# Lightning attention and a low-rank mixer on one core: the attention steps regrouped by TensorE tile shape

## The chip, the cores and the metric

The kernel runs on one core of one Trainium2 chip. The metric is the device time of one execution in microseconds (us). Of the kernel before there are three runs, 670.92, 672.37 and 673.74 us, so the median is 672.37 us.

## The reference

Two blocks follow each other. The first is causal linear attention with a decay per head, on q, k, v of 4 batches, 8 heads, 768 tokens and 64 columns. The reference does it by blocks of 64 tokens; in short:

```python
for each block of tokens:
    intra = ((q k^T) * Dmask) v            # Dmask = lam^(i-j) for i >= j, else 0
    inter = (q * lam^(pos+1)) kv_state
    out   = intra + inter
    kv_state = lam^block * kv_state + (k * lam^(block-1-pos))^T v
```

The heads' columns are put side by side, which gives x of 4 x 768 tokens x 512 columns. The second block mixes tokens through a product of rank 32 and then has a layer over the columns:

```python
h   = x^T @ U @ V                          # over the 768 tokens, rank 32
u   = x + h^T
out = u + max(u @ w_ch1, 0) @ w_ch2        # 512 -> 2048 -> 512
```

Everything is float32 in and out.

## The kernel before

Attention takes 128 tokens of one batch a step, all eight heads at once: 24 steps s, six to a batch (NT = 6, c = s % NT is the step's place in its batch). In a step the heads lie in pairs (HP = 4 pairs a, x = 0 or 1 within the pair), and `half` is the upper or lower 64 partitions. Its parts are:

- `prep(s)`: TensorE transposes q and k (L355, into pq and pk), four 128x128 transposes each, and ScalarE copies the results to qt and kt (L358). Step 0 does it in two parts.
- `scale(s)`: GpSimd makes qs = qt times powers of the decay (L383), and ks, the scaled keys of the next step (L372).
- `scores(s)`: products of kt and qt into the two banks pss (L400); for s over 6 on tiles of 64x64, before that of 64x128.
- `masked(s)`: VectorE multiplies pss by the decay mask, one instruction for each x, into sm (L409).
- `inter(s)`: qs times the state kv into the two banks px, on 64x64 tiles (L441); not in a batch's first step.
- `intra(s)`: sm times v, added into the same px, on 128x64 tiles (L453); ScalarE then copies px to xs[s], the step's 128x512 piece of x (L459).
- `state(s)`: ks times v into the bank pkv (L418); VectorE adds the faded old state to give kv[s + 1] (L424, L426). `fade` is the fading, four ScalarE instructions (L392). A batch's last step has no state.

Behind the attention, by seven steps, runs the mixer's first part on finished batches. `low(b)` forms U^T x of a whole batch in pp (L470). `low_rows(b)` and the three pieces that `next_of_low(b)` runs one by one split its rows into a high and a low part and spread them over four groups of 32 partitions of p_hl (L490, L496, L501, L505). `mix(s)` multiplies by V and VectorE adds the sum onto xs[s], which makes it u (L515, L518). `turn(s)` transposes u (L532), stores u to DRAM on the SP queue (L535), and VectorE splits the transposed u in two parts (ut L537, u_hl L548); `turned` is the rest of that split, on ScalarE (L551) and GpSimd (L552).

Beside this, `aside(s)` runs single pieces of the preparation of weights (U, V and the first column blocks of w_ch1): VectorE instructions (L149 to L224, L615 to L626), with ScalarE ones that are held back in a list and issued at `late` (L167, L168, L212).

The order of all instructions in this stage is written out by hand, in the list `pieces` (L562 to L584); each engine takes its own in that order. For the steady step it gives TensorE: transposes of q and k of s + 1, mix, intra(s), state(s), scores(s + 1), inter(s + 1), transposes of u. PSUM has eight banks: pss and px two each, and one each with the tags pq, pk, pu and pt. Loads of q, k and v are issued on the SP queue where a buffer is freed (q and v have three, k four).

After the last attention step come the first product (`hidden`, L733 and L743), into which the last batch's turns and mixes are put at written slots (the list `rest`, L788), and the second product (`product`, L866 to L870). Both use fp32r matmuls of 128x128 by 512 columns.

## Time and profile before

| what | value |
|---|---|
| median of three runs | 672.37 us |
| profiled execution | 671.76 us, span 669.9 us, TensorE clock 1.00 |
| start of the first product (L733) | 119.06 us |
| 0 to 119.06 us, busy | TensorE 116.84, VectorE 96.76, ScalarE 76.63, GpSimd 70.58 us; DMA share 0.86 |
| 119.06 to 144 us, busy | TensorE 24.94, VectorE 21.44, ScalarE 13.63 us |
| 144 us to the end, busy | TensorE 522.13 of 525.90, VectorE 379.29 us |

A matmul's record contains its way through the array, so that records of a stream overlap; what one costs in a stream is the time from one start to the next. The chain of work that ended last gives such times for a run of instructions: a line has its start, the time it held the chain, the engine, the tile written, the line of the code and the number of records. The page and the list of groups give per group the number of records, busy time and mean duration, and behind the bar the engine's idle time just ahead of them. In the order of time a line shows start, length from first start to last end, engine, line and operation, and the tiles.

### The profile page before, as it was taken

How to read it: one execution, taken by the hardware profiler on the slowest of the kernel's cores; microseconds unless marked ns; L12 is line 12 of the kernel's file. 1: busy time of each engine (PE TensorE's matmuls, PEld its weight loads, DVE VectorE, ACT ScalarE, POOL GpSimd, SP SyncE). 2: the span in 40 equal slices, each digit the busy share in tenths (PEclk: the TensorE clock that was granted, in tenths of full speed). 3: DMA queues.
4: the chain of work that ended last, by engine and by line, in shares of the span. 5: the costliest groups of instructions: out<-in, count | busy, mean ns of one | idle time of the engine just before them, and what ended most of it. 6: DMA issues, size and time to landing. Idle time of an engine off the chain costs nothing.

```text
span 669.9 us, 13328 instructions
## 1 busy us (share of the span) xinstructions
PE 663.9 (99%) x5204; PEld 544.5 (81%) x5204; DVE 497.5 (74%) x873; ACT 277.5 (41%) x517; POOL 112.1 (17%) x92
## 2 busy tenths in 40 slices
PE   9999999999999999999999999999999999999997
PEld 8898989788888888888888888888888888888886
DVE  4689989877999777777797265787586775865864
ACT  4675866454655444444454122232322322322320
POOL 4455767240000000000000000030030300300300
PEclk9999999999999999999999999999999999999999
DMA  8999894354776655555577989854363353543421
GB/s 188 219 234 248 212 246 141 102 196 153 262 251 233 215 202 202 201 202 204 204 282 273 326 308 392 282 184 136 95 220 95 118 196 95 160 155 94 163 90 63
DMA packets 131776, 131.29 MB, mean 196 GB/s; under 512 B 81346, under 2 KB 89794, under 8 KB 131714
## 3 DMA queue, kind: packets, MB, share of 16 engines
q1 hardware_dynamic: 130512, 130.05, 61.1%
q8 instruction: 41, 0.67, 0.4%
q10 hardware_dynamic: 1202, 0.39, 0.2%
q14 instruction: 21, 0.17, 0.1%
HBM read 80.09 MB, written 50.33 MB: 195 GB/s over the span
## 4 chain that ended last, share of the span: by engine, by line
PE 97%; DVE 1%; DMA 1%; ACT 0%; issue 0%; DVEq 0%; ACTq 0%
PE pz L733 27%; PE pz L868 13%; PE pz L866 13%; PE pd L743 13%; PE pd L870 13%; PE px L453 4%; PE pss L400 3%; PE put L532 2%; PE pq L355 2%; PE pkv L418 1%; PE pk L355 1%; PE px L441 1%; DMA qraw<-in_q_dram 1%; PE pp L470 1%; PE pu L515 1%; PE idle L343 0%
## 5 line engine op out<-in xcount | busy, mean ns | idle before, releaser
L733 PE MATMUL pz<-u_hl,w 128*128 128x512 f32 x768 | 190.5, 397 | 0.0
L733 PEld LDWEIGHTS pz<-u_hl,w 128*128 128x128 f32 x768 | 144.0, 188 | 35.4 <-issue 0.4
L868 PE MATMUL pz<-w_hl,m 128*128 128x512 f32 x384 | 151.1, 396 | 0.0
L866 PE MATMUL pz<-w_hl,m 128*128 128x512 f32 x384 | 150.9, 396 | 0.0
L870 PE MATMUL pd<-w_d,m 128*128 128x512 f32 x384 | 149.5, 396 | 0.0
L849 ACT ACTIVATE m<-mt 128x512 fp32r<-128x512 f32 x96 | 60.5, 632 | 196.4 <-PE pd L870 140.9
L850 DVE SCALAR_TENSOR_TENSOR m<-rm,m 128x512 fp32r<-128x512 f32 x96 | 71.4, 746 | 53.8 <-ACT m L849 53.5
L895 POOL TENSOR_TENSOR o<-o,u 128x512 f32<-128x512 f32 x20 | 29.9, 1527 | 447.4 <-DVE o L891 447.4
L748 DVE SCALAR_TENSOR_TENSOR r<-pd,r 128x512 f32<-128x512 f32 x96 | 61.8, 686 | 53.6 <-ACT r L739 43.5
L743 PE MATMUL pd<-u_d,w 128*128 128x512 f32 x384 | 98.6, 397 | 0.0
L739 ACT ACTIVATE r<-pz 128x512 f32<-128x512 f32 x96 | 52.2, 596 | 93.2 <-PE pz L733 92.5
L868 PEld LDWEIGHTS pz<-w_hl,m 128*128 128x128 f32 x384 | 72.3, 188 | 17.7
L870 PEld LDWEIGHTS pd<-w_d,m 128*128 128x128 f32 x384 | 72.3, 188 | 17.6
L866 PEld LDWEIGHTS pz<-w_hl,m 128*128 128x128 f32 x384 | 72.3, 188 | 17.6
L743 PEld LDWEIGHTS pd<-u_d,w 128*128 128x128 f32 x384 | 72.1, 188 | 17.3
L851 DVE SCALAR_TENSOR_TENSOR m<-m 128x512 fp32r<-128x512 f32 x96 | 69.1, 721 | 0.9
L848 DVE TENSOR_SCALAR mt<-rm 128x512 uint32<-128x512 uint32 x96 | 46.1, 481 | 26.4 <-DMA rm<-r_d 26.1
L409 DVE TENSOR_TENSOR sm<-pss,mask 128x512 f32<-128x512 f32 x48 | 30.9, 685 | 7.3 <-PE pss L400 7.1
L212 ACT CAST w<-wt 128x512 fp32r<-128x512 f32 x32 | 19.9, 620 | 30.6 <-DVE wt L209 23.4
L383 POOL TENSOR_TENSOR qs<-qt,powq 128x512 f32<-128x512 f32 x20 | 25.9, 1297 | 20.3 <-ACT qt L358 19.8
L453 PEld LDWEIGHTS px<-vraw,sm 128*64 128x64 f32 x768 | 24.6, 137 | 5.5 <-issue 2.3
L453 PE MATMUL px<-vraw,sm 128*64 128x64 f32 x768 | 28.1, 225 | 0.1
(88 smaller groups left out, 682.1 us busy)
## 6 DMA issues: line engine op xcount, KB each, us to landing
r_d<-r SPq DMA_DIRECT2D x96, 256.0 KB, 2.4
rm<-r_d SPq DMA_DIRECT2D x96, 256.0 KB, 2.7
words<-in_moe_w_ch_dram SPq DMA_DIRECT2D x30, 512.0 KB, 4.5
w_d<-w SPq DMA_DIRECT2D x16, 768.0 KB, 3.3
w_hl<-w_d SPq DMA_DIRECT2D x16, 512.0 KB, 6.3
vraw<-in_v_dram SPq DMA_DIRECT2D x24, 256.0 KB, 5.0
u_d<-x_nat SPq DMA_DIRECT2D x24, 256.0 KB, 3.7
u<-u_d SPq DMA_DIRECT2D x24, 256.0 KB, 4.0
```

What stands on the lines that cost most here:

```text
L453: nc.tensor.matmul(out=px[half[t], x, a, :], lhsT=sm[:, x, a, half[t]], rhs=vr[:, 2 * a + x, :], start=(first and a == 0), stop=(a == HP - 1),
L733: nc.tensor.matmul(out=acc[g][0], lhsT=w[:, n, ct, :], rhs=uhl[g][:, n, ct, :], start=(ct == 0 and n == 0), stop=(ct == CT - 1 and n == 1),)
L739: nc.scalar.mul(rs[g], acc[g][0], 4096.0 + 1.0)
L743: nc.tensor.matmul(out=acc[g][1], lhsT=w[:, 2, ct, :], rhs=ud[g][:, ct, :], start=(ct == 0), stop=(ct == CT - 1),)
L748: nc.vector.scalar_tensor_tensor(rs[g], acc[g][1], 4096.0, rs[g], ALU.mult, ALU.add)
L848: nc.vector.tensor_scalar(t.bitcast(U32), r.bitcast(U32), HI, None, ALU.bitwise_and)
L849: nc.scalar.activation(out=m[:, 0], in_=t, func=AF.Relu)
L850: nc.vector.scalar_tensor_tensor(m[:, 1], r, 0.0, hi, ALU.max, ALU.subtract)
L851: nc.vector.scalar_tensor_tensor(m[:, 2], hi, E, low, ALU.mult, ALU.subtract)
L866: nc.tensor.matmul(out=pz, lhsT=m[:, 0, cols], rhs=hl[:, 0], start=first, stop=False)
L868: nc.tensor.matmul(out=pz, lhsT=m[:, 1, cols], rhs=hl[:, 1], start=False, stop=end)
L870: nc.tensor.matmul(out=pd, lhsT=m[:, 2, cols], rhs=dd, start=first, stop=end)
```

## The change

What it does, part by part:

- Transposes of q, k and (in the attention stage) u are done by halves of the tokens: each takes 64 partitions to 128, on a 64x128 tile, with the two halves written to two different banks. There are sixteen for q and k and eight for u in place of eight and four. q and k share the two banks `pqk`.
- `scores` uses 64x128 tiles in all steps.
- `mix` is four matmuls of 64 rows and 256 columns. p_hl holds the rows of the first 256 columns in its upper half and those of the others in its lower half, and the columns of p_hl hold the high and the low part. The sum is added onto xs by `mixed`, apart from the matmuls.
- `turn` and `mix` share two banks `pm`: the left half holds the transposes, the right half the sums. `turn` is one step later than before and works on the piece mixed a step earlier. Its two VectorE instructions are issued by `split`, and `store` is the DMA of u.
- `intra` comes first on px and is ordered by x; `inter(s)` follows `state(s)` in the same step, adds onto intra's sums and ends with the copy to xs.
- `state` writes to the first of the banks `pqk`.
- `low(b)` runs at the end of the batch's last step, in the banks px, and (but for the last batch) is followed by four ScalarE copies of its rows; `low_rows` works on 32x512 and the lows on 32x256 pieces.
- The mix of the batch's last piece before the first product (piece 17) moves from the first product into the last attention step. The turn of piece 16 moves from slot 4 to slot 7 of the first product.

The core of the diff:

```diff
-    def turn_half(s, a0, name):
-
-        ts, tag = (qts, ("pq", "pt")) if name == "q" else (kts, ("pk", "pu"))
+    def turn_parts(s, a0):
+
+        n = HP // parts(s)
         if a0 == 0:
-            ts[s] = att.tile([P, HP, P], FP32, tag=name + "t", bufs=2, name=name + "t")
-        n = HP // parts(s)
-        pt = one_bank([P, n, P], "p" + name, tag[a0 > 0])
-        for a in range(a0, a0 + n):
-            nc.tensor.transpose(
-                out=pt[:, a - a0, :], in_=raw[s, name][:, 2 * a : 2 * a + 2, :], identity=ident
-            )
-        nc.scalar.copy(ts[s][:, a0 : a0 + n, :], pt)
+            for ts, name in ((qts, "qt"), (kts, "kt")):
+                ts[s] = att.tile([P, HP, P], FP32, tag=name, bufs=2, name=name)
+        pt = two_banks("pqk", "px" if a0 else "pqk")[:, :, 0 : 2 * n * D]
+        pt = pt.rearrange("p t (n a i) -> p t n a i", n=2, a=n)
+        for i, name in enumerate("qk"):
+            for a in range(n):
+                for t in range(2):
+                    nc.tensor.transpose(
+                        out=pt[:, t, i, a, :],
+                        in_=raw[s, name][half[t], 2 * (a0 + a) : 2 * (a0 + a) + 2, :],
+                        identity=ident[half[t], half[t]],
+                    )
+        for i, ts in enumerate((qts, kts)):
+            nc.scalar.copy(
+                ts[s][:, a0 : a0 + n, :].rearrange("p a (t i) -> p t a i", t=2), pt[:, :, i]
+            )

     def prep(s):
         for a0 in range(0, HP, HP // parts(s)):
-            for name in "qk":
-                turn_half(s, a0, name)
+            turn_parts(s, a0)
...
-                for rows in half if s > NT else [slice(0, P)]:
-                    nc.tensor.matmul(
-                        out=pss[rows, x, a, :], lhsT=kt[half[x], a, rows],
-                        rhs=qt[half[x], a, :], start=True, stop=True,
-                    )
+                nc.tensor.matmul(
+                    out=pss[:, x, a, :], lhsT=kt[half[x], a, :], rhs=qt[half[x], a, :],
+                    start=True, stop=True,
...
-            pkv = one_bank([P, HP, D], "pkv", "pk")
+            pkv = two_banks("pkv", "pqk")[:, 0, 0 : HP * D].rearrange("p (a e) -> p a e", a=HP)
...
-    def inter(s):
+    def intra(s):

         st[s]["px"] = both = two_banks("px", "px")
         px = both[:, :, 0 : HP * D].rearrange("p x (a e) -> p x a e", a=HP)
-        if s % NT == 0:
-            return
-
-        for a in range(HP):
+        sm, vr, alone = st[s]["sm"], raw[s, "v"], s % NT == 0
+        for x in range(2):
+            for a in range(HP):
+                for t in range(2):
+                    nc.tensor.matmul(
+                        out=px[half[t], x, a, :], lhsT=sm[:, x, a, half[t]],
+                        rhs=vr[:, 2 * a + x, :], start=(a == 0), stop=(alone and a == HP - 1),
+                    )
+
+    def inter(s):
+
+        px = st[s]["px"][:, :, 0 : HP * D].rearrange("p x (a e) -> p x a e", a=HP)
+        for a in range(HP if s % NT else 0):
             for x in range(2):
                 for t in range(2):
                     nc.tensor.matmul(
                         out=px[half[t], x, a, :], lhsT=st[s]["qs"][half[x], a, half[t]],
-                        rhs=kv[s][half[x], a, :], start=(a == 0), stop=False,
-                    )
-
-    def intra(s):
-        first = s % NT == 0
-        sm, vr, px = st[s]["sm"], raw[s, "v"], st[s]["px"]
-        px = px[:, :, 0 : HP * D].rearrange("p x (a e) -> p x a e", a=HP)
-        for a in range(HP):
-            for x in range(2):
-                for t in range(2):
-                    nc.tensor.matmul(
-                        out=px[half[t], x, a, :], lhsT=sm[:, x, a, half[t]],
-                        rhs=vr[:, 2 * a + x, :], start=(first and a == 0), stop=(a == HP - 1),
+                        rhs=kv[s][half[x], a, :], start=False, stop=(a == HP - 1),
                     )
         pool, tag = (att, "x10") if s % 10 == 5 else (x_pool, "x")
         xs[s] = pool.tile([P, C], FP32, tag=tag, name="x_nat")
         nc.scalar.copy(xs[s].rearrange("p (a x e) -> p x a e", a=HP, x=2), px)
-
+        del st[s]
...
-        tag = "pq" if b else "pu"
-        pp = one_bank([P, P], "pp", tag) if b < B - 1 else bank([P, P], "pp", "b2")
+        pp = two_banks("pp", "px")[:, 0, 0:P] if b < B - 1 else bank([P, P], "pp", "b2")
         for c in range(NT):
             for g in range(G):
                 nc.tensor.matmul(
@@ -472,53 +473,100 @@
                     rhs=xs[b * NT + c][:, g * P : (g + 1) * P],
                     start=(c == 0), stop=(c == NT - 1),
                 )
-        pps[b] = pp
+        if b == B - 1:
+            pps[b] = pp
+            return
+        pps[b] = rows_f = tmp("p_f")[0:R]
+        for g in range(G):
+            nc.scalar.copy(rows_f[:, g * P : (g + 1) * P], pp[g * R : (g + 1) * R])
...
+        rows_f = pp
+        nc.vector.tensor_scalar(t.bitcast(U32), rows_f.bitcast(U32), HI, None, ALU.bitwise_and)
+        wide = [slice(x * 2 * P, (x + 1) * 2 * P) for x in range(2)]
+
+        def place(g, low):
+            return p_hl[g * R : (g + 1) * R, wide[low]]
+
+        def spread():
+            for g in range(G):
+                nc.scalar.copy(place(g, 0), t[:, wide[g // 2]])

         def low_part():
-            for rows, cols in own:
+            for x in range(2):
                 nc.vector.tensor_tensor(
-                    out=l[:, cols], in0=pp[rows], in1=t[:, cols], op=ALU.subtract
+                    out=place(2 * x, 1), in0=rows_f[:, wide[x]], in1=t[:, wide[x]],
+                    op=ALU.subtract,
                 )

-        def spread():
-            nc.scalar.copy(h, t)
-            nc.scalar.copy(h2, t)
-
         def spread_low():
-            nc.scalar.copy(l2, l.bitcast(FP32))
+            for x in range(2):
+                nc.scalar.copy(place(2 * x + 1, 1), place(2 * x, 1).bitcast(FP32))

         pps[b] = [spread, low_part, spread_low]

...
+    def both_halves(s):
+        if s not in pms:
+            pms[s] = two_banks("pm", "pqk" if s == NS - NT - 1 else "pm")
+        return pms[s]
+
     def mix(s):
         b, c = divmod(s, NT)
-        pu = one_bank([P, C], "pu", "pu") if s < NS - NT - 1 else bank([P, C], "pu", "b2")
-        nc.tensor.matmul(
-            out=pu, lhsT=v_hl[:, c * P : (c + 1) * P], rhs=p_hl, start=True, stop=True
-        )
+        weights = v_hl[:, c * P : (c + 1) * P]
+        if b < B - 1:
+            pm = both_halves(s)[:, :, 2 * P :]
+            for low in range(2):
+                for x in range(2):
+                    nc.tensor.matmul(
+                        out=pm[:, x], lhsT=weights[half[x]],
+                        rhs=p_hl[half[x], low * 2 * P : (low + 1) * 2 * P],
+                        start=(low == 0), stop=(low == 1),
+                    )
+            return
+        pu = bank([P, C], "pu", "b2")
+        nc.tensor.matmul(out=pu, lhsT=weights, rhs=p_hl, start=True, stop=True)
         nc.vector.tensor_tensor(out=xs[s], in0=pu, in1=xs[s], op=ALU.add)
+
+    def mixed(s):
+        pm, x = pms.pop(s)[:, :, 2 * P :], xs[s].rearrange("p (x e) -> p x e", x=2)
+        nc.vector.tensor_tensor(out=x, in0=pm, in1=x, op=ALU.add)

+    def store(s):
+        nc.sync.dma_start(out=u_d[s], in_=xs[s])

...
-        nc.vector.tensor_tensor(out=low, in0=pt, in1=t, op=ALU.subtract)
+        pt = both_halves(s + 1)[:, :, 0 : 2 * P].rearrange("p t (c i) -> p t c i", i=D)
+        for ct in range(CT):
+            for n in range(2):
+                nc.tensor.transpose(
+                    out=pt[:, n, ct, :], in_=xs[s][half[n], ct * P : (ct + 1) * P],
+                    identity=ident[half[n], half[n]],
+                )
+        del xs[s]
...
+        t = tmp("ut").rearrange("p (c n) -> p c n", n=P)
+        split_t = parts_of(t.bitcast(U32))
         turned[s] = rest

-
-
-
-
-    pieces = [("prep", 0), ("scale", 0), ("scores", 0), ("inter", 0), ("masked", 0)]
+        def split():
+            nc.vector.tensor_scalar(split_t, pt.bitcast(U32), HI, None, ALU.bitwise_and)
+            nc.vector.tensor_tensor(
+                out=parts_of(low), in0=pt, in1=parts_of(t), op=ALU.subtract
+            )
+
+        splits[s] = split
+
+    splits = {}
+
+    pieces = [("prep", 0), ("scale", 0), ("scores", 0), ("masked", 0)]
     for s in range(NS):
         b, c = divmod(s, NT)
         done = s - NT - 1
         more = s + 1 < NS
-        step = [("prep", s + 1), ("scale", s + 1)] * more + [("fade", s)] * (c == 1)
+        turns = done > 0 and (done - 1) // TG < FG
+        mixes = 0 <= done < NS - NT - 1
+        step = [("prep", s + 1), ("scale", s + 1)] * more
+        step += [("turn", done - 1)] * turns + [("mix", done)] * mixes
+        step += [("mix", done + 1)] * (not more)
+        step += [("next_of_low", b - 1)] * (c == 0 and b > 0)
+        step += [("fade", s)] * (c == 1)
         step += [("late", s - 1)] * (s in (NT, 3 * NT - 1))
-        step += [("mix", done)] * (0 <= done < NS - NT - 1)
-        step += [("low", b - 1)] * (c == 0 and b > 0)
-        step += [("low_rows", b - 1)] * (c == 0 and b > 0)
-        step += [("intra", s)]
+        step += [("split", done - 1)] * turns + [("next_of_low", b - 1)] * (c == 0 and b > 0)
+        step += [("mixed", done)] * mixes + [("mixed", done + 1)] * (not more)
         step += [("next_of_low", b - 1)] * (c == 0 and b > 0)
-        step += [("late", s)] * (s < NT - 1 or s == NT) + [("state", s)]
-        step += [("next_of_low", b - 1)] * (c == 0 and b > 0)
+        step += [("intra", s), ("state", s), ("inter", s)]
+        step += [("late", s)] * (s < NT - 1 or s == NT)
         step += [("turned", done - 1)] * (done > 0) + [("late", s)] * (done >= 0)
-        step += [("next_of_low", b - 1)] * (c == 0 and b > 0)
         step += [("scores", s + 1)] * more
+        step += [("low", b)] * (more and c == NT - 1)
         step += [("aside", s)] * (s >= 2 * NT)
-        step += [("inter", s + 1), ("masked", s + 1)] * more
+        step += [("masked", s + 1)] * more
+        step += [("low_rows", b)] * (more and c == NT - 1)
         step += [("fade", s + 1)] * (more and c > 0)
         step += [("aside", s)] * (s < 2 * NT)
-        step += [("turn", done)] * (done >= 0 and done // TG < FG)
+        step += [("store", done)] * (done >= 0 and done // TG < FG)
         pieces += step
...
+    pl = two_banks("pl", "pss")[:, 0, 0:H]
     keep_busy(2)
-    pl = one_bank([P, H], "pl", "pt")
...
-        (0, 4, "turn", c0 - 2), (0, 6, "mix", c0 - 1), (0, 9, "low", b), (0, 14, "low_rows", b),
+        (0, 7, "turn", c0 - 2), (0, 9, "low", b), (0, 14, "low_rows", b),
```

For the last batch, `low_rows`, `mix` and `turn` keep their old form inside the first product.

## The prediction

> **What bounds the kernel now.** I read the page first, for which engine fills the span:
>
> ```profile
> span 669.9 us, 13328 instructions
> PE 663.9 (99%) x5204; PEld 544.5 (81%) x5204; DVE 497.5 (74%) x873; ACT 277.5 (41%) x517; POOL 112.1 (17%) x92
> ```
>
> TensorE carries 97% of the chain that ended last. By the chain, the first product (L733) starts at 119.06 us; only what lies before it, and one mix just after, is touched. From 144 us on TensorE has no gap and runs the same matmuls in both kernels. So the next view is the chain, one attention step at a time:
>
> ```profile
> 78.16 0.59 PE put L532 x4
> 78.75 0.44 PE pq L355 x4
> 79.18 0.44 PE pk L355 x4
> 79.62 0.23 PE pu L515
> 79.85 1.08 PE px L453 x32
> 80.93 0.47 PE pkv L418 x16
> 81.40 1.19 PE pss L400 x32
> 82.59 0.51 PE px L441 x31
> ```
>
> A step is TensorE end to end; the neighbouring one (73.42 to 78.16) has 1.03 and 0.46 in the last two rows and makes 4.74 us. Like work costs 0.59 when it follows another tile shape (put) and 0.44 when it doesn't: a change of shape is 0.15 us, and the step has three (into put, px L453, pss).
>
> Next the groups by shape, for the durations of one:
>
> ```profile
> L355 PE MATMUL pq<-ident,qraw 128*128 128x128 f32 x96 | 15.5, 284 | 0.3 <-DMA qraw<-in_q_dram 0.2
> L400 PE MATMUL pss<-qt,kt 64*128 64x128 f32 x112 | 8.9, 305 | 0.0
> L400 PEld LDWEIGHTS pss<-qt,kt 64*128 64x128 f32 x112 | 7.6, 207 | 0.7 <-ACT kt L358 0.3
> ```
>
> One fp32 matmul leaves two records, a transpose one. In the early steps the scores already use the 64*128 shape: sixteen records whose weight loads last 207 ns each take 1.09 us with the shape change, so the two row halves overlap.
>
> Last, who is next in line. VectorE's instructions of the same step in order of time:
>
> ```profile
> 78.34 1.28 DVE L409 TENSOR_TENSOR sm<-pss,mask 128x512 f32<-128x512 f32 x2
> 79.54 0.68 DVE L537 TENSOR_SCALAR ut<-put 128x512 uint32<-128x512 uint32 x1
> 80.25 0.69 DVE L548 TENSOR_TENSOR u_hl<-put,ut 128x512 fp32r<-128x512 f32 x1
> 80.86 0.68 DVE L518 TENSOR_TENSOR x_nat<-pu,x_nat 128x512 f32<-128x512 f32 x1
> 81.52 0.42 DVE L426 TENSOR_TENSOR kv<-pkv,faded 128x256 f32<-128x256 f32 x1
> 81.86 0.68 DVE L224 SCALAR_TENSOR_TENSOR w<-wt,w 128x512 fp32r<-128x512 f32 x1
> ```
>
> and ScalarE's of step 9:
>
> ```profile
> 51.24 0.58 ACT L459 COPY x_nat<-px 128x512 f32<-128x512 f32 x1 [0.63 <-PE px L453]
> 51.72 0.64 ACT L551 ACTIVATE u_hl<-ut 128x512 fp32r<-128x512 f32 x1
> 52.25 0.71 ACT L167 ACTIVATE sc<-sc,vp 128x512 f32<-128x512 uint32 x1
> 53.00 0.72 ACT L168 ACTIVATE sc<-sc,vp 128x512 uint32<-128x512 f32 x1
> 53.63 1.05 ACT L392 ACTIVATE faded<-kv,powq 128x64 f32<-128x64 f32 x4
> 54.58 0.56 ACT L358 COPY qt<-pq 128x512 f32<-128x512 f32 x1
> ```
>
> From start to start VectorE needs 1.20 (two masks) + 0.71 + 0.61 + 0.60 + 0.38 = 3.5 us a step, and the weight pieces of `aside` come on top: 0.42 to 1.54 us in most steps. It is 4.0 to 5.0 in a 4.74 us step: VectorE is close behind TensorE.
>
> **What the Trainium skill says.** "TensorEngine Tiling (Array Packing)", Key Properties: changing the tiling mode drains TensorE; the trace agrees with 0.15 us each. "TensorE: Matmul & The Clock Gate", Part 3, What overlaps: a weight load overlaps matmuls in flight when the row group differs; the early scores agree, 68 ns a record at most against loads of 207. The same page, Part 1: ScalarE and VectorE take their queues strictly in order; the ScalarE lines above keep the program's order. No page prices an fp32 transpose of half the rows.
>
> **The change part by part.** *Transposes by halves.* Before, twelve a step, 0.44/4 = 109 ns each. After, 24, each with 64 moving columns instead of 128, alternating row halves, each half into its own bank. If columns set the pace and halves overlap: 109/4 = 27 ns. If halves take turns: 55. If columns don't matter: 109. I take 29, since the scores overlap in the same shape, alternating in the same way: 16 x 29 = 0.46 for q and k (was 0.88), 8 x 29 = 0.23 for turn (was 0.59 with its shape change). *Mix* as four fp32r matmuls of 64 rows and 256 columns: the same streaming, 0.24 against 0.23. *Intra, state*: 1.08 and 0.47 as before. *Inter* pays a shape change of its own: 0.62, as the early steps show in "px L441" after 64*128 scores. *Scores* on 64*128: 1.09. Sum: 0.46+0.23+0.24+1.08+0.47+0.62+1.08 = 4.18, or 0.56 less than 4.74. Three shape changes stay three.
>
> *Cover of the masks.* Masks start 0.06 after the scores end; their two halves are ready 0.80 and 1.40 us after it. Today 2.16 us of TensorE work (inter, put, pq, pk, pu) hide that; then 0.46+0.23+0.24 = 0.93. Intra is now ordered by x, so its first half starts at 1.07 (0.80 needed) and its second at 1.54 (1.40 needed): still hidden, by 0.14. Steps 1 to 5 have only prep, 0.46: intra ends 1.91 after the scores, and the step is 1.91+0.47+0.62+1.08 = 4.08 against 4.29.
>
> *VectorE* keeps its 3.5 us, so a step costs the larger of 4.18 and 3.5 plus its aside: split and mixed are the same three passes over 128x512, only in other order.
>
> *ScalarE and the shared banks.* pkv now lies in the banks of prep's transposes, so state(s) waits for kt(s+1), and prep(s+2) waits for VectorE's kv(s). Behind inter(s) ScalarE has xs 0.48, hi 0.53, fade 0.95, qt 0.47, kt 0.57: with latencies 3.11 us until state(s+1) may start; TensorE gets there in 1.08+0.93+1.08 = 3.09. Balanced, where nothing else is in ScalarE's queue. In step 9 the exponents (L167, L168: 0.75+0.63) stand there: state(10) waits 1.4 us more. The one for U in step 2 costs about 0.3.
>
> *The low-rank rows.* low(b) moves to the end of step c=5; VectorE's low_rows stands behind the mask and waits for four ScalarE copies (1.06, the row p_f<-pp) after low's 1.45+0.14. VectorE stands idle there up to 1.4 us, with the aside, split and kv behind it; it saves about 0.9 by working on 32x512 and 32x256 pieces instead of 32x128 ones (0.41+1.19 against 1.23+1.25). For b=0 there is no such saving, and 1.9 us of aside (L626) queue behind the wait.
>
> *DMA* stays: the same loads and stores, the u_d store at the same end of the step, released by mixed earlier in the same step. Loads have three to four buffers, three steps of 4.2 us, and land in 4.3 to 5.0 (6.6 at most). Cover is ample; without it a late load would cost what qraw did once at the start, 0.4. GpSimd's three (qs, ks, u_d: 1.30+1.06+1.42 = 3.8 a step) keep their order; qs is now needed a step later than it is made, so they fit under 4.2.
>
> **The sum**, over starts of the masks (L409). Before, 7 to 8 up to 22 to 23: 3.95, 4.73, 4.74, 4.74, 4.66, 6.81, 4.37, 5.00, 4.34, 4.76, 4.27, 6.54, 4.63, 4.73, 4.34, 4.73 us. After, by the rules above: steps 1 to 5, -0.2 three times (one waits for q's DMA) and +0.3: -0.3. 5 to 6 is VectorE's: 0. 6 to 7, +0.65 (low_rows ahead of L626). 7 to 8, 4.18: +0.2. 8 to 9 and 9 to 10, 4.18 and 4.20: -1.1. 10 to 11, 5.6: +0.86. 11 to 14: VectorE holds it by the 1.54 us aside (L186), then by low_rows; 15.5 against 15.84: -0.3. 14 to 15, 3.5+1.22: -0.25. 15 to 16, VectorE: 0. 16 to 17 and 17 to 18, 4.20 and 3.75: -1.1. 18 to 21, low_rows and asides of 1.2: +0.1. 21 to 22: -0.15. 22 to 23: -0.5. Step 23 and one mix less in the first product: -0.2. Together -1.8 to -1.9 us. The profiled execution had 671.76 around its span of 669.9, 0.6 below the median of 672.37; I take the difference off the median: 670.5.
>
> **Rivals.** *A: VectorE isn't the wall.* Its asides were stretched by GpSimd (L178 took 0.59 from start to start once and 1.18 another time), and ScalarE may get through sooner. Then most steps are 4.2: about -0.5 in 14 of them, -7 us, 665.5. Against: VectorE is busy 26.76 of 28.30 us from 62.3 to 90.6.
> *B, the other side: the halves don't overlap*, in prep and turn. At p ns each the step is 3.49+24p; at 55 it is 4.81, which is over the present 4.74 and over what VectorE needs in nearly all steps. By the same list that is +3.7 us, 676; at 109, 6.1 us a step, 697. It decides beyond about 53 ns. For: no 64-row transpose is in the trace. Against: the 64*128 scores.
> *C: ScalarE's loop is longer than balanced*, 0.3 us more in each of nine fade steps and low_rows another 0.5 three times: +4 on the forecast, 674.5.
> *D: nothing moves*, a loop I have missed sets 4.74: 672.4. I see none.
>
> **How the numbers follow.** Forecast (PE shorter, most given back) 0.45, its own range 667.5 to 673.5; A 0.19; B 0.17 (two thirds of it near 676 to 682); C 0.15; D 0.04. Half a per cent, 3.4 us, is about what a measurement can tell here (the three runs span 670.92 to 673.74); the borders are 669.0 and 675.7. Faster: A and 0.3 of the forecast, 0.33. Slower: 0.15 of B, half of C, and 0.05 for the forecast's own tail, 0.28. Same 0.39. The range takes in A and C and the nearer part of B: 664 to 680.
>
> **What would show it.** Right: L355's successor at about 29 ns from start to start, a shortest step near 4.2, VectorE at 9 tenths through the stage, idle weight loads of intra put down to sm, and of pkv to kt, the latter longest near the exponents after step 9. First product near 117. Wrong: transposes of 55 ns or more (B); VectorE with gaps in every step (C); steps of 4.2 throughout (A).

## The result, and the profile after

The changed kernel takes 675.85 us (median of five runs, 674.07 to 676.69) against 671.54 us for the kernel before in the same session (five runs, 670.70 to 673.74): a ratio of 1.0056, with a 95% interval of 1.0031 to 1.0082. It is slower by about 4 us, where 1.9 us less were predicted. The profiled execution took 676.67 us around a span of 674.9.

The head of the page of the changed kernel, with the busy time of each engine:

```profile
span 674.9 us, 13392 instructions
PE 659.7 (98%) x5242; PEld 541.2 (80%) x5242; DVE 500.4 (74%) x864; ACT 280.0 (41%) x534; POOL 111.9 (17%) x92
```

TensorE has 4.2 us less to do than before (659.7 against 663.9), and the span is 5.0 us longer. So the work did get shorter, and TensorE has 9.2 us more of idle time (15.2 against 6.0). The first product starts at 124.46 us (119.06 before). From there to the end it is 550.4 us against 550.8. Everything lost was lost in the attention stage.

One step of it in the chain of work that ended last (start, time, engine, tile and line):

```profile
48.15 0.49 PE pqk L358 x16
48.65 0.25 PE pm L600 x8
48.90 0.29 PE pm L551 x4
49.19 1.08 PE px L444 x32
50.27 0.47 PE pkv L424 x16
50.74 0.62 PE px L455 x32
51.36 1.12 PE pss L406 x16
```

Sixteen transposes of half the tokens for q and k take 0.49 us, 31 ns each, and the eight of turn (L600) 0.25 us, 31 ns each. The step is 4.30 us where it was 4.74. But few steps come at this pace. The next fence is the waits of TensorE up to 125 us (in total, times, longest):

```profile
PE pqk L358 <- DVE kv L430: 5.3, 3, 2.1
PE pqk L358 <- DVE kv L432: 1.4, 2, 1.0
```

The first line is the larger. Three times, in the first step of a batch (steps 6, 12 and 18, where kv is a plain copy, L430), TensorE stops before the next transposes until VectorE has copied the state kv: for 1.70 us (until 42.38), 2.06 (74.25) and 1.58 (103.75). Before, the three such places showed nothing: from 20 us on, the only wait listed for another engine was 0.6 us, elsewhere:

```profile
PE put L532 <- DVE x_nat L518: 0.6, 1, 0.6
```

The cause is VectorE's queue. These are its instructions around the second of these waits, in order of time, with the idle time ahead of one in brackets:

```profile
66.69 1.29 DVE L415 TENSOR_TENSOR sm<-pss,mask 128x512 f32<-128x512 f32 x2
69.25 0.41 DVE L511 TENSOR_SCALAR p_h<-p_f 32x512 uint32<-32x512 uint32 x1 [1.27 <-ACT p_f L481]
...
71.51 1.63 DVE L523 TENSOR_TENSOR vp<-p_f,p_h 32x256 fp32r<-32x256 f32 x2
73.18 0.69 DVE L563 TENSOR_TENSOR x_nat<-pm,x_nat 128x512 f32<-128x512 f32 x1
73.78 0.41 DVE L430 COPY kv<-pkv 128x256 f32<-128x256 f32 x1
```

`low_rows` (L511) waits for ScalarE's four copies with the whole queue behind it, and `low_part` (L523) now stands ahead of `mixed` (L563) and of kv (L430). In the kernel before the order in this step was `low_rows`, kv, and only then the lows:

```profile
65.88 1.22 DVE L490 TENSOR_SCALAR p_h<-pp 32x128 uint32<-32x128 uint32 x4
67.23 0.42 DVE L424 COPY kv<-pkv 128x256 f32<-128x256 f32 x1
67.69 1.25 DVE L496 TENSOR_TENSOR vp<-pp,p_h 32x128 fp32r<-32x128 f32 x4
```

Because pkv now lies in the bank that the next transposes write, a late kv stops TensorE.

What can follow such a stop shows in windows of 1 us around and behind the first of them (busy time and instructions of PE, PEld, DVE, ACT, POOL, then the granted clock, DMA share, GB/s):

```profile
41.00:42.00 1.00, 0.00 (x0) 0.00 (x0) 0.94 (x3) 0.89 (x3) 0.15 (x1) 1.00 0.26 59
44.00:45.00 1.00, 1.00 (x24) 1.00 (x22) 0.51 (x1) 0.97 (x4) 1.00 (x1) 0.50 0.97 219
```

After a stretch with no matmul the granted clock is 0.50 from 43 to 46 us, and lower than 1.00 in the two windows around, and step 7 to 8 takes 5.96 us. No window of the kernel before is below 0.99. The other two waits of this execution had no such sequel.

Last, ScalarE in the steps with a fade:

```profile
116.23 0.58 ACT L461 COPY x_nat<-px 128x512 f32<-128x512 f32 x1 [1.48 <-PE px L455]
116.72 0.64 ACT L607 ACTIVATE u_hl<-ut 128x512 fp32r<-128x512 f32 x1
117.25 1.05 ACT L399 ACTIVATE faded<-kv,powq 128x64 f32<-128x64 f32 x4
118.21 0.56 ACT L364 COPY qt<-pqk 128x512 f32<-128x512 f32 x1
118.67 0.59 ACT L364 COPY kt<-pqk 128x512 f32<-128x512 f32 x1
```

The next copy of px starts at 120.73, so the step has 4.50 us. ScalarE works without a gap from 116.23 to 119.26 and then waits 1.48 us for inter, which stands behind state, which needs the bank that the copy of kt reads. It is a ring through two engines, 0.20 us longer than TensorE's own 4.30.

### The profile page after: what moved, and what is told of

Same layout as the page of the kernel before. It is cut to its first block, busy times and chain, and to the rows that moved or that the text cites. A ratio compares the mean times of both kernels' runs of the same rounds, so it can differ in the third digit from the quotient of the medians.

```text
span 674.9 us, 13392 instructions
## 1 busy us (share of the span) xinstructions
PE 659.7 (98%) x5242; PEld 541.2 (80%) x5242; DVE 500.4 (74%) x864; ACT 280.0 (41%) x534; POOL 111.9 (17%) x92
## 4 chain that ended last, share of the span: by engine, by line
PE 93%; DVE 3%; issue 1%; SPq 1%; ACT 1%; DMA 1%; DVEq 0%
PE pz L806 27%; PE pz L941 13%; PE pz L939 13%; PE pd L816 13%; PE pd L943 13%; PE px L444 3%; PE pss L406 2%; PE px L455 2%; PE pqk L358 1%; PE pkv L424 1%; PE pp L471 1%; SPq L279 1%; DVE vp L523 1%; PE pm L551 1%; DMA qraw<-in_q_dram 1%
## 5 line engine op out<-in xcount | busy, mean ns | idle before, releaser
L444 PEld LDWEIGHTS px<-vraw,sm 128*64 128x64 f32 x768 | 26.1, 141 | 4.3 <-ACT faded L399 0.9
```

The costliest lines, as they stand in the source:

```text
L444: nc.tensor.matmul(out=px[half[t], x, a, :], lhsT=sm[:, x, a, half[t]], rhs=vr[:, 2 * a + x, :], start=(a == 0), stop=(alone and a == HP - 1),
```

## The experiments

All runs but the one on the kernel before start from the changed kernel. Times are medians, with the ratio to the kernel before of the same session (671.8 to 672.0 us, in the last session 673.12). "7 to 8" is the time between the first masks of steps 7 and 8.

**Whole transposes.** The new order, banks and mix stay; q, k and u are transposed in 128x128 pieces again.

```diff
-                for t in range(2):
-                    nc.tensor.transpose(out=pt[:, t, i, a, :],
-                        in_=raw[s, name][half[t], ...], identity=ident[half[t], half[t]])
+                nc.tensor.transpose(out=pt[:, i, a, :], in_=raw[s, name][...], identity=ident)
...
```

> Changed kernel with the transposes of q, k and u undone to whole 128x128 ones in the same banks and at the same places in the order (q in the first bank, k in the second). Theory (halves cost 31 ns each, whole ones 109; where VectorE and ScalarE don't hold the step it is TensorE's): a step's TensorE work rises from 4.30 to about 5.1, of which the steps held by VectorE (about 5.0) absorb most; about 0.8 us in nine steps and 0.2 in the others, +8 us, 684. Rival (VectorE holds all steps, the faster transposes were worth nothing): within 2 us of 675.9.

685.87 us, 1.0206 (1.0173 to 1.0239). Its chain:

```profile
120.17 1.02 PE pqk L357 x8
121.19 0.44 PE pm L596 x4
121.63 0.43 PE pm L548 x4
```

Against 0.49, 0.25 and 0.29 this is 0.86 us a step, and the late steps take 5.16 us, TensorE end to end. So 31 ns fit halves that overlap, as predicted (55 was summed for halves that take turns), and in this order they are worth 10 us. The loss lies elsewhere. The mix's 0.43 instead of 0.29 (0.14 more) comes where it now follows transposes of another tile shape.

**The change profiled a second time**, with nothing edited.

> The changed kernel once more, for a second profile. Theory (TensorE's halt of 1.2 us in step 1, for which the profile names no cause, and the lateness of the first scores belong to one execution's start, while the loads come in): mask 2 starts between 16.3 and 17.3 as in the other variants, not at 17.73, and without that halt; the low clock near 43 us comes again. Rival (the changed order makes the halt): it is there again, within 0.3 us.

677.72 us, 1.0083 (1.0057 to 1.0109), five runs from 674.74 to 680.30; the profiled one (674.74, span 672.9) was the shortest. The three waits for kv are there again (5.3 us), but the clock is 1.00 throughout, 7 to 8 takes 4.52 us instead of 5.96, and a stop of 1.2 us in step 1 of the first profile, for which no wait is shown, is gone. So these two belong to single executions. The rest of the loss, first product at 122.51, is in both. From here on intervals are compared with the second profile.

**Rows of `low` behind the weight piece.**

```diff
-        step += [("low_rows", b)] * (more and c == NT - 1)
         step += [("fade", s + 1)] * (more and c > 0)
         step += [("aside", s)] * (s < 2 * NT)
+        step += [("low_rows", b)] * (more and c == NT - 1)
```

> Changed kernel with one line moved: in steps below 12, low_rows is listed after aside instead of ahead of it, so that VectorE does U's and V's pieces while ScalarE copies the low-rank rows. Theory (low_rows stands in VectorE's queue and waits for ScalarE): the interval between masks 6 and 7 falls from 6.76 to about 5.9, that between 12 and 13 from 7.43 to about 6.9, the whole by 1.3 us from the changed kernel's 675.85. If the lower TensorE clock after the gap goes too, another 1.3. Rival (VectorE is full there anyway, the wait only shifts): no more than 0.3 us.

674.19 us, 1.0036 (1.0025 to 1.0047). 6 to 7 falls from 6.70 to 5.97 us and 12 to 13 from 7.42 to 6.95; 18 to 19, where no weight piece could move ahead, stays at 6.94. VectorE now does the weight piece while ScalarE copies.

**Filling TensorE's wait.** Matmuls that nobody reads, put into the first gap (six of 128x128), and into it (four) together with the later rows. The function `fill` that issues them is left out of the excerpt.

```diff
+        step += [("fill", 6)] * (s == NT)
         step += [("low", b)] * (more and c == NT - 1)
```

> Changed kernel with six more fp32 128x128 matmuls of the identity into the free banks pm, after the scores of step 7, at the place where TensorE stood idle for 1.7 us before step 7. They add no needed work. Theory (the gap lets the granted clock fall to 0.50 for some 3 us, in which step 7's intra takes 1.90 instead of 1.08): clock 1.00 in steps 7 and 8, the interval from mask 7 to mask 8 falls from 5.96 to about 4.6, the whole by 1.3 us. Rival (step 7 is slow for want of data, not clock): the interval stays at 5.9 and the time at 675.9 or a little more.

> Both edits at once, low_rows after aside and four filling matmuls. Theory: the gains add, 2.4 us less than the changed kernel, about 673.4, and the first product starts near 122. Rival: the second edit adds nothing once the gap is shorter, about 674.5 at best.

675.77 us, 1.0058 (1.0036 to 1.0080), and 674.12 us, 1.0038 (1.0027 to 1.0049): like the change and like the later rows alone. The wait in the first gap shrank to 0.22 us in the first of them, but 6 to 7 stayed at 6.70. The clock stayed at 1.00 in both profiles, but it did so without filling in the second profile of the change too, so a profile alone tells nothing here. The mean granted clock of every run does: 4 of the 8 runs with six matmuls lie at 0.996 or 0.997, as 6 of the 10 of the change do (0.994 to 0.997), against 2 of 17 with later rows alone and 2 of 18 with both. Filling this one gap did not keep the clock up; the other two stops were still there.

**Fade behind the copies of q and k**, in the step that uses it.

```diff
-        step += [("fade", s)] * (c == 1)
+        step += [("fade", s)] * (c > 0)
...
-        step += [("fade", s + 1)] * (more and c > 0)
```

> Changed kernel with each fade issued in its own step behind the copies of q and k, and no longer at the end of the step before, ahead of them. Theory (ScalarE's xs, hi, fade, qt, kt stand one behind the other, and state, now in the transposes' banks, waits for kt: 4.50 us a turn): the steps of 4.50 become 4.30, those from 15 to 16 about 4.4; -1.8 us against the changed kernel. Rival (VectorE holds these steps too): -0.3 us.

675.19 us, 1.0053 (1.0038 to 1.0067). The late steps fall from 4.50 to 4.30 us, which is TensorE's own time, 15 to 16 from 4.78 to 4.25, and 10 to 11 from 5.08 to 4.70. So the ring through ScalarE was real. 5 to 7 lose 1.0 us again (4.79 and 7.12 against 4.19 and 6.70), in steps whose ScalarE and VectorE queues hold other weight pieces.

**Rows a whole step later**, without and with the fade's move.

```diff
+        if c == 0 and b > 0:
+            step += [("low_rows", b - 1)] + [("next_of_low", b - 1)] * 2
...
-        step += [("low_rows", b)] * (more and c == NT - 1)
```

> Changed kernel with low_rows and the first two pieces of next_of_low behind mixed, in the step after low, and the third behind turned. Theory (VectorE stands idle 0.9 to 1.3 us for ScalarE's copies in steps 6, 12 and 18, and everything behind it waits): the intervals 6 to 7, 12 to 13 and 18 to 19 fall by 0.9, 1.2 and 1.0, the clock stays up after 6; -3 us against the changed kernel, half of it regained at worst by the later steps. Rival (the ScalarE chain that follows takes it back): -0.5 us.

> The last two edits together. Theory: they act in different steps and add, -4.8 us against the changed kernel, about 671, within half a per cent of the kernel before on either side. Rival (something else holds most steps): no better than 674.

681.72 us, 1.0144 (1.0124 to 1.0164), and 678.85 us, 1.0103 (1.0086 to 1.0120). The expectation was wrong: 12 to 13 falls only to 7.15, while 13 to 14 and 19 to 20 rise to 7.53 and 8.19 (8.29 and 7.61 with the fade's move), with a clock of 0.50 from about 75 and 105 us on (from 71 and 105 with the fade's move). In the first of the two TensorE still waits 1.78 us for kv, twice, and the mix waits 0.83 us more for the copy of `spread_low` (until 74.42), so the delay reaches into the next step.

**Filling in all three waits**, written to the second, idle bank of pkv's tile: alone, with rows and fade moved, and then those moves without the filling. In the last two ScalarE and VectorE share the four copies. The excerpt shows only where the filling is issued.

```diff
+        step += [("fill", s)] * (c == 0 and s > 0)
```

> Changed kernel with seven fp32 128x128 matmuls of the identity behind the scores of steps 6, 12 and 18, into the second, then idle bank of pkv: they fill the three stretches of 1.7 to 2.1 us in which TensorE waits for kv before the next transposes. Theory (such a stretch can halve TensorE's clock for 3 to 7 us, at one or another of the three places from run to run, which is why the changed kernel's runs lie between 674.1 and 680.3 and its profiles between 672.9 and 674.9 of span): no clock below 1.00 in the profile, runs within 3 us of each other, median 673.5 to 674.5. Rival (the scatter comes from the loads at the start): the scatter and the median of 676 to 677 stay.

> Changed kernel with low_rows behind aside in steps below 12, each fade from step 7 on in its own step, two of the four row copies of low_rows on VectorE behind the mask instead of ScalarE, and five filling matmuls at the three stretches. Theory: -0.9 and -0.5 (low_rows), -0.2 in seven steps (fade), -0.4 at two places (copies), and a clock that stays up: about 671, equal to the kernel before within 0.3%. Rival (the edits get in each other's way as low_rows and fade did before): 673 or more.

> The same without the filling matmuls. Theory: the stretches are now 1.2 to 1.6 us, short enough for the clock in most runs, so 671 to 672, at most 1 us more than with them. Rival (the clock still falls in half of the runs): 673 or more, with a wider scatter.

682.43 us, 1.0152 (1.0130 to 1.0173); 677.18 us, 1.0076 (1.0057 to 1.0095); 674.42 us, 1.0035 (1.0023 to 1.0048). The filling failed as a test. Written to the tile that kv is read from, it had to wait for kv itself, as TensorE's waits in the first of them show:

```profile
PE pkv L350 <- DVE kv L438: 5.4, 3, 2.1
```

So it came after the gap and only added to the path. The run without it says more: with rows and fade moved, two waits of 1.72 us for kv remained (until 71.35 and 99.98), and behind the second 102 to 104 had a clock of 0.50 and 19 to 20 took 6.17 us. Behind the first the clock stayed up.

**A gap in the kernel before.** Five memsets of 128x512 on VectorE, ahead of the masks of steps 13 and 19, with no other edit; they add no needed work.

```diff
+        step += [("idle", s)] * (s in (2 * NT, 3 * NT))
         step += [("inter", s + 1), ("masked", s + 1)] * more
```

> The kernel before with five VectorE memsets of a 128x512 scratch tile ahead of the masks in steps 12 and 18, to make TensorE wait there: a stretch of about 2 us twice. Theory (it is the wait, not the changed kernel's instructions, that halves the clock): the profile shows 0.50 behind at least one of the two, and that place costs 1.5 us over the delay itself; together 5 to 8 us over the kernel before. Rival (the clock falls for another reason): 1.00 throughout, and only the delay of about 2 us twice, +4.

679.44 us, 1.0116 (1.0092 to 1.0141). TensorE's line at the first gap, and a window of 1 us behind it:

```profile
71.63 1.61 PE L457 MATMUL px<-vraw,sm 128*64 128x64 f32 x18 [2.15 <-DVE sm L413]
```

```profile
73.00:74.00 1.00, 1.00 (x26) 1.00 (x23) 1.00 (x2) 0.00 (x0) 0.00 (x0) 0.50 0.92 266
```

The old instructions lose their clock in the same way: 0.50 for three windows behind each of the two gaps of 2.15 us. The two gapped intervals are 2.81 us longer each, and the steps behind them lose another 2.6 us (13 to 15: +1.00 and +0.14; 19 to 21: +0.88 and +0.58). All four runs have a mean clock of 0.994 to 0.997, where no run of the kernel before is below 0.999. So such a gap cost more than its length, and the halves are not needed for it.

**kv ahead of `low_part`.** The order of the kernel before, restored: split, mixed, kv, and then the lows, with spread_low behind turned.

```diff
-        step += [("split", done - 1)] * turns + [("next_of_low", b - 1)] * (c == 0 and b > 0)
+        step += [("split", done - 1)] * turns
         step += [("mixed", done)] * mixes + [("mixed", done + 1)] * (not more)
-        step += [("next_of_low", b - 1)] * (c == 0 and b > 0)
         step += [("intra", s), ("state", s), ("inter", s)]
+        step += [("next_of_low", b - 1)] * (c == 0 and b > 0)
...
         step += [("turned", done - 1)] * (done > 0) + [("late", s)] * (done >= 0)
+        step += [("next_of_low", b - 1)] * (c == 0 and b > 0)
```

> The changed kernel with low_part moved to the end of its step: VectorE does split, mixed and kv first, the 32x256 passes after them; spread_low behind turned. Nothing is left out. Theory (TensorE waits because low_part stands ahead of kv, and the next prep needs kv): the two waits of about 2.1 us in steps 12 and 18 shrink below 1 us, no window falls under a granted clock of 0.95, intervals 12 to 13 and 18 to 19 shorten by up to 1 us each, the steps behind them stay near 4.5; about 673.5 us against 675.9 for the change. Rival (VectorE's work, not its order, sets the intervals): 12 to 13 and 18 to 19 stay at 7.4 and 6.9, or what they lose comes back as a wait of mix for spread_low in 13 to 14 and 19 to 20; no better than 675 us.

673.11 us, 1.0023 (1.0009 to 1.0036). The same step of VectorE:

```profile
71.90 0.42 DVE L430 COPY kv<-pkv 128x256 f32<-128x256 f32 x1
72.23 0.85 DVE L523 TENSOR_TENSOR vp<-p_f,p_h 32x256 fp32r<-32x256 f32 x2
73.11 1.29 DVE L415 TENSOR_TENSOR sm<-pss,mask 128x512 f32<-128x512 f32 x2
```

`low_part` itself is shorter here: 0.85 us for its two passes against 1.63 in the change. There GpSimd was multiplying when they started (ks, 71.37 to 72.42); here its ks had ended at 72.21:

```profile
71.37 1.05 POOL L379 TENSOR_TENSOR ks<-kraw,small 128x512 f32<-128x512 f32 x1
```

TensorE's waits for kv at L430 shrink from 5.3 us in three to 0.4 in one, 12 to 13 falls from 7.42 to 6.63, 18 to 19 from 6.94 to 6.36, no window is below a clock of 0.99, and none of its 8 runs has a mean clock below 0.999. So the gain holds both the shorter waits and the clock that they no longer pull down. The steps behind give little back: 13 to 14 falls to 4.29, and the mix waits 1.0 us in all for spread_low's copy. In this profile, of the longest of the 8 runs, the first product is still late by stops of 0.91 and 0.71 us between masks 2 and 5 with no wait shown.

**All three moves together**: rows behind the weight piece, fade in its own step from step 7 on, kv ahead of low_part. The excerpt has the first two; the third is the edit above.

```diff
-        step += [("fade", s)] * (c == 1)
+        step += [("fade", s)] * (c == 1 or s > NT)
...
-        step += [("low_rows", b)] * (more and c == NT - 1)
-        step += [("fade", s + 1)] * (more and c > 0)
+        step += [("fade", s + 1)] * (0 < s < NT)
         step += [("aside", s)] * (s < 2 * NT)
+        step += [("low_rows", b)] * (more and c == NT - 1)
```

> The run above with two moves more: low_rows behind aside (as in the run with rows late) and fade behind the copies of q and k from step 7 on (as in the run on fade). Nothing is left out. Theory: the three gains add, 1.7 us from low_rows, 2.5 us from fade in the steps from 7 on, 2 us from the order of low_part: 670 to 672 us, level with the kernel before. Rival: they share one limit, VectorE, and the sum stays at 673.5 to 675 us, as in the run that joined rows and fade with no filling (674.4).

670.74 us (21 runs), 0.9986 (0.9976 to 0.9995). Of the 4 us, all are back and one more, and no window is below 0.99. It differs from the run with rows and fade moved and no filling (674.42 us) by the order around kv and by who makes the four copies; and 10 of that run's 19 executions have a mean clock of 0.997 or less, none of these 21 has less than 0.999. From mask 20 on its steps are 4.30 us one after another. One place pays: in 7 to 8 (4.97 us) the mix waits 1.01 us for spread_low's copy, which now stands behind turned.

**The weight pieces of steps 6 to 11 ahead of the mask**, on top of this.

```diff
-        step += [("aside", s)] * (s >= 2 * NT)
+        step += [("aside", s)] * (s >= NT)
         step += [("masked", s + 1)] * more
...
-        step += [("aside", s)] * (s < 2 * NT)
+        step += [("aside", s)] * (s < NT)
```

> The run with all three moves (rows, fade, low_part) and one more: the weight pieces (aside) of steps 6 to 11 stand ahead of the mask instead of behind it, so that split, mixed and kv come sooner behind the mask. Nothing is left out. Theory (VectorE's stretched pass L149 in step 9, 1.50 us ahead of split, makes 9 to 10 last 5.28 us): the pass goes into the time in which VectorE waits for the scores, 9 to 10 falls to 4.3 to 4.8 and the kernel to about 670 us, against 670.7. Rival: the pass then stands ahead of a mask that is ready, intra waits for the mask instead of prep for kv, and the sum of 6 to 12 stays within 0.5 us: 670.5 to 671.5 us.

671.43 us against 673.12, 0.9978 (0.9966 to 0.9989). In the change a piece in step 9 took 1.49 us on VectorE while GpSimd's multiplication for qs ran:

```profile
54.04 1.28 POOL L390 TENSOR_TENSOR qs<-qt,powq 128x512 f32<-128x512 f32 x1
54.11 1.49 DVE L149 TENSOR_SCALAR m<-words 128x512 uint32<-128x512 uint32 x1
```

Behind it kv came late, and TensorE waited 0.96 us for it (until 57.91), the longer of the two waits at L432. Moved, it falls between two of GpSimd's multiplications (ks until 49.98, u_d from 50.66) and takes 0.41, as in the kernel before:

```profile
50.18 0.41 DVE L149 TENSOR_SCALAR m<-words 128x512 uint32<-128x512 uint32 x1
```

The Trainium skill, "SBUF — State Buffer", SBUF: two separate sides, says that GpSimd and VectorE contend for a port which they share; these times agree, though no run here shows the port itself. The wait for kv in step 9 is gone too. But 9 to 10 still took 5.18 us (5.28 without the move): in this profile TensorE stopped for 0.66 us in the middle of state's matmuls, for no wait that is shown. The sum from 6 to 12 is 29.1 us against 29.0 without the move, so the rival's figure came about, for another reason than the rival's. The two ratios' intervals overlap; that this last move helps is not shown. That the whole is faster than the kernel before, by 0.1 to 0.2 per cent, is: both intervals lie below 1.

## Why the prediction was wrong

The prediction's list, added up, gives -2.1 us and not the -1.9 that it states; its last entry, -0.2 for step 23 and the mix, doesn't fit into the stated sum. This changes nothing below. The times between masks, as the prediction divided them, against the kernel before (us):

| steps | predicted | change, first profile | second profile | with all moves (last run) |
|---|---|---|---|---|
| start to mask 1 | not summed | -0.66 | -0.52 | +0.20 |
| 1 to 5 | -0.3 | +2.13 | +0.92 | +1.14 |
| 5 to 6 | 0 | -0.02 | -0.02 | -0.01 |
| 6 to 7 | +0.65 | +1.45 | +1.39 | +0.60 |
| 7 to 8 | +0.2 | +2.01 | +0.57 | +1.02 |
| 8 to 10 | -1.1 | +0.11 | +0.72 | +0.01 |
| 10 to 11 | +0.86 | +0.34 | +0.34 | +0.17 |
| 11 to 14 | -0.3 | +0.12 | +0.13 | -1.09 |
| 14 to 15 | -0.25 | -0.27 | -0.27 | -0.44 |
| 15 to 16 | 0 | +0.44 | +0.44 | -0.09 |
| 16 to 18 | -1.1 | -0.69 | -0.69 | -0.90 |
| 18 to 21 | +0.1 | +0.24 | +0.24 | -0.69 |
| 21 to 23 | -0.65 | -0.07 | -0.08 | -0.47 |

Up to mask 23 the second profile is 5.1 us above the prediction's list, and no single step of it makes up most of that: the three stretches with low-rank rows (6 to 7, 11 to 14, 18 to 21) hold 1.3, 8 to 10 hold 1.8, 1 to 5 hold 1.2, and the steps in which ScalarE's ring sets the pace (15 to 18, 21 to 23) 1.4; the rest is smaller and of both signs.

**Right: TensorE's step.** Transposes of 31 ns (29 predicted), inter 0.62, scores 1.09 to 1.12, intra 1.08, state 0.47; the mix is 0.29 instead of 0.24. The step is 4.30 where 4.18 was summed. The transposes show that rival B is out. Where TensorE sets the step, that is 0.12 more than predicted.

**Wrong: the step on the low-rank rows.** The prediction saw `low_rows` wait up to 1.4 us (1.27 measured) and named the aside, split and kv behind it. It then charged this as VectorE's time alone, with a saving of 0.9 for larger pieces. The saving was 0.4: `low_rows` and `low_part` took 0.41 and 1.63 where 0.41 and 1.19 were entered, against 1.22 and 1.25 before. And it overlooked that `low_part` had moved from behind kv to ahead of it, although the prediction itself says that the next transposes wait for kv. That is two lines of the diff in the order of pieces. Its list has +0.65, -0.3 and +0.1 for the three stretches, where the second profile has +1.39, +0.13 and +0.24, with TensorE waiting 5.3 us for kv in them. Putting kv ahead alone took the median from 675.85 to 673.11 us, more than half of the loss, and 12 to 13 and 18 to 19 below what they take in the kernel before (6.63 and 6.36 against 6.81 and 6.54).

**Wrong: what a stop of TensorE costs.** No term stood for the clock. The Trainium skill, "TensorE: Matmul & The Clock Gate", Part 1: The HAM clock gate, says that the clock falls to half after an idle window of about 3.4 us that runs freely. The half is what the traces show; the length is not: stops of 1.70 to 2.15 us sufficed here in some executions and not in others, and the measurement decides. It cost 1.4 us in step 7 of the first profile and nothing in the second. How often it came is seen from the mean granted clock of each run, which is at least 0.999 in every run of the kernel before that lists it:

| longest stop of TensorE in the profile, from mask 1 on | kernels | runs with a mean clock of 0.998 or less |
|---|---|---|
| 1.71 to 2.15 us | the change, whole transposes, first wait filled, fade moved, rows a step later (two), filling in all waits (two), rows and fade without filling, gap in the kernel before | 44 of 68 |
| 1.58 us | rows behind the weight piece, without and with filling | 4 of 35 |
| 0.91 to 1.17 us | kv ahead of `low_part` (three) | 0 of 43 |

So the clock fell more often where the stops were longer, and in none of the 43 runs of kernels whose profiles show stops of 1.17 us at most. The stops are those of one execution of each kernel, so this gives no exact border. In the change the six runs at 0.997 or less have a median of 676.68 us and the four others 674.85: by this estimate the clock is worth about 1.8 us to a run that it meets, and 3 us of the loss remain without it.

**Mis-sized: ScalarE's ring.** "Balanced" at 3.11 against 3.09 was 0.2 short: the fade steps have 4.50 us where TensorE needs 4.30. Moving the fade returned 0.20 us in the late steps and 0.53 in 15 to 16. Rival C had this mechanism (0.3 us in nine fade steps, low_rows three times more), at 674.5 us; it had neither the kv queue nor the clock. Rival B's figure of 676 is nearer to the measured 675.85, by luck, since its mechanism is out. The exponents of step 9 were the other way off: +0.34 against +0.86 in 10 to 11.

**Wrong: steps 8 to 10** by the neighbour of a weight piece: 1.49 us for 0.41 beside GpSimd, and TensorE's wait of 0.96 us behind it. 9 to 10 took 5.28 us in both profiles where 4.20 was predicted; in the second profile a stop of 0.34 us with no wait shown lies in 8 to 9 besides. The prediction had seen such a stretch (0.59 and 1.18 for one line) as a reason for being faster, not as a risk of a new order.

**Wrong: steps 1 to 5.** 0.9 us more in the second profile where -0.3 was predicted. The plain step was summed as 4.08; the shortest that the profiles show here is 4.26, with 0.57 for state and 1.16 to the end of the scores where 0.47 and 1.08 were entered. Two more parts stand in both profiles. Between masks 3 and 4 (4.81 us) ScalarE does the exponents of U, the fade and the copies of q and k without a gap, in the second profile until 23.18, and state starts at 23.27: the prediction's own term for U, at 0.3, came out at 0.55. Between masks 4 and 5 (4.50 us) two weight pieces were again stretched beside GpSimd (qs and ks, 26.92 to 30.88), and kv and the mask followed them without a pause:

```profile
27.20 1.43 DVE L149 TENSOR_SCALAR m<-words 64x384 uint32<-64x384 uint32 x1
28.66 1.30 DVE L178 SCALAR_TENSOR_TENSOR m<-words,m 64x384 f32<-64x384 uint32 x1
```

In the kernel before the same two took:

```profile
27.00 0.35 DVE L149 TENSOR_SCALAR m<-words 64x384 uint32<-64x384 uint32 x1
27.38 0.55 DVE L178 SCALAR_TENSOR_TENSOR m<-words,m 64x384 f32<-64x384 uint32 x1
```

The rest differs from profile to profile: waits for a load of q (0.29 us in the second profile) and a stop with no shown wait in the first (1.17 us, until 16.33). About the same excess stayed with all moves (+1.14). What TensorE waits for in these stops, which come at other places in each profile (step 1, 2 or 9), stays open. In two of them (the one in step 1 and the 0.66 us of the last run) no packet of the queues of the kind instruction was on its way.

With the moves the total comes near the forecast, -1.1 and -1.7 us timed against -1.9, but not by the forecast's steps: in the last column the time to mask 11 is 3.1 us longer than in the kernel before, and from there to mask 23 it is 3.7 us shorter.

## What to carry to other kernels

- When a buffer gets a second user, follow that user's wait back through the whole queue of the engine that frees the buffer: work that is cheap in itself (two passes, 0.85 us together, 1.63 beside GpSimd) was part of a stop of 2 us on another engine once it stood ahead of the copy that frees the bank.
- Shortening the bound engine's step by a tenth shows the next rings, each shorter by little. List them before: here ScalarE's 4.50 against 4.30, and VectorE's queue at the turn from one batch to the next. Reordering the queues, with not one instruction less, was worth 5 us and turned the sign of the change.
- A new order gives every instruction new neighbours. Passes of VectorE that met a GpSimd multiplication took up to 1.49 us for 0.41; a sum of the durations seen in the old order misses that.
- A gap in TensorE's work costs its length and sometimes a slow clock behind it; compare several executions before reading a step time from one, and their mean clocks.

## What the runs showed that was not expected

- A granted clock of 0.50 for three windows of 1 us and parts of two more (longer in the runs with the rows a step later) behind stops of 1.70 to 2.15 us, in the kernel before too once it was given such stops; in repeated executions of one kernel it comes behind some stops and not behind others, less often behind 1.58 us (2 of 17 runs) than behind 1.7 to 2.1 (6 of 10).
- A 128x512 pass of VectorE that took 0.41 us alone and 1.49 us beside a GpSimd multiplication; the same between masks 4 and 5, and in `low_part`.
- TensorE stops of 0.4 to 1.2 us for which the profile shows no wait, at other places in each execution.
